# The 96-column remainder of the gate and up projections with x stationary and both weights moving, turned back by a DMA transpose

## The chip, the cores and the metric

The kernel runs on one core of one Trainium2 chip. The metric is the device time of one execution in microseconds (us), given as the median of several runs. The core has a matrix engine (TensorE; PE in the profile, with its weight loads listed apart as PEld), VectorE (DVE), ScalarE (ACT), GpSimd (POOL) and SyncE (SP, whose queue issues nearly all DMAs here). The profile lists each engine's instructions in order of time and, from semaphore events, which engine ended each wait. PSUM is the memory that the matmuls write (PS in the profile); a DMA has *landed* when its data has arrived.

Ratios are the mean time of one kernel's fast runs over the mean of the kernel before in the same rounds on the same chip, so they are not quite the ratio of the medians beside them.

## The reference, cut to what matters

```python
def _B_ref(x, w_gate, w_up, w_down):            # S = 2048 rows, D = 512, F = 1376
    return (_gelu(x @ w_gate) * (x @ w_up)) @ w_down
xn = _layernorm(x)
return x + _A_ref(xn, ...) + _B_ref(xn, w_gate, w_up, w_down)   # _A_ref: a state-space scan
```

F = 1376 is ten tiles of 128 columns and a remainder of 96. The change concerns that remainder in `x @ w_gate` and `x @ w_up`.

## The kernel before

The 2048 rows are worked in four blocks of 512. A gate/up stage computes the hidden layer *transposed*: F on the partitions, rows on the free axis, as the down projection needs it as its stationary operand. A weight tile is stationary (128 columns, or 96 for tile 10) and 512 rows of x move past it. The 96-column tile costs as much as a full one: the trace below has 88 matmuls of 512 moving columns in a stage at 216 ns each, the 8 with 96 stationary columns included.

```python
def GU(b, fts=None):                            # gate/up stage of block b
    def mm(ft, W, Wc, bank, c0, c1, rd):
        m = FROWS[ft]                           # FROWS = [128] * 10 + [96]
        def f(e):
            for dk in range(KD):                # KD = 4: D = 4 * 128
                ins_ = e.matmul(PS[bank][0:m, c0:c1], W.ap[:, dk, 128 * ft:128 * ft + m],
                                XNT[b].ap[:, dk, c0:c1], start=(dk == 0), stop=(dk == KD - 1))
    ... # [cut]
    for ft in fts:
        banks[ft] = (next_bank(), next_bank())  # 8 PSUM banks in turn
        kk = (KF * b + ft) % 3                  # KF = 11; three GG and three UPB buffers
        ... # [cut: 2 x 4 matmuls of 512 moving columns]
        ACT(... GG[kk] <- Gelu(PS[bg]) ...)     # "gelu"
        ACT(... UPB[kk] <- PS[bu] ...)          # "evU"
        V(... HTt[k2][ft] <- GG[kk] * UPB[kk] ...)   # "hmul" on DVE

def TR(b):                                      # input of block b, transposed by DMA
    for j, tt in enumerate(range(4 * b, 4 * b + 4)):
        S.dma(... e.dma_start_transpose(XNT[b].ap[:, :, 128*j:128*(j+1)], XN[tt % 8].ap) ...)

# order of the stages (BU: input of the scan, CHAIN: the scan on DVE, DN: down projection)
GU(0, range(5, KF)); ... BU(1); ... CHAIN(1)
GU(1, range(0, 8)); TR(2); GU(1, range(8, KF)); BU(2); CHAIN(2); DN(0, True)
GU(2, range(0, 8)); TR(3); GU(2, range(8, KF)); BU(3); CHAIN(3); DN(1)
GU(3); DN(2); DN(3)
```

A scheduler in the kernel orders the instructions of ACT, DVE and POOL by priority, but keeps PE and the SP queue in program order (`INORDER = ("tensor", "sync")`). Where a DMA stands in the program text is therefore where it stands in the SP queue.

Of the kernel before, what the change touches and what calls it, by code (L numbers as in the profile page):

```python
# [9 lines left out]
ALU = mybir.AluOpType  # L10
ACTF = mybir.ActivationFunctionType
BF16, F32, I32 = dt.bfloat16, dt.float32, dt.int32
# [332 lines left out]
L, D, P, F = 2048, 512, 512, 1376  # L345
NT, NB, KD, KP, KF = 16, 4, 4, 4, 11
TB_ = 512
FROWS = [128] * 10 + [96]
# [4 lines left out]
def d_pe(n_list):  # L353
    return sum(n / 2.4 + 2.5 for n in n_list)
def d_dve_tt2x(n): return 100.0 + 0.52 * n
def d_dve_1x(n): return 100.0 + 1.04 * n
def d_dve_scan(n): return 90.0 + 2.08 * n
def d_dve_ts4x(n): return 220.0 + 0.26 * n
D_TINY = 160.0
def d_act(n, ptr=0): return 190.0 + 0.833 * n + 90.0 * ptr  # L360
# [3 lines left out]
def build(nc, ins, out):  # L364
    with ExitStack() as es:
        E = es.enter_context
        S = Sched(nc, es)
        ARENA_BYTES = 207 * 1024
        arena_t = E(nc.sbuf_tensor("arena", [128, ARENA_BYTES // 2], BF16))
        A = Arena(arena_t, ARENA_BYTES)  # L370
        PS = [E(nc.psum_tensor("PS%d" % i, [128, 512], F32)) for i in range(8)]
        BANK = [Buf("bank%d" % i, "ps", i, i + 1) for i in range(8)]

        def ring(parent, name, n):
            return [A.sub(parent, "%s%d" % (name, i), i) for i in range(n)]

        WG = A.alloc("WG", [KD, F], BF16)
        WU = A.alloc("WU", [KD, F], BF16)
        WD = A.alloc("WD", [KF, D], BF16)
        FCH = [(0, 384), (384, 896), (896, F)]  # L380
        WGc = [Buf("WGc%d" % i, "sbx", 10 * i, 10 * i + 1) for i in range(3)]
        WUc = [Buf("WUc%d" % i, "sbx", 100 + 10 * i, 101 + 10 * i) for i in range(3)]
        WDc = [Buf("WDc%d" % i, "sbx", 200 + 10 * i, 201 + 10 * i) for i in range(2)]
        XNT_all = A.alloc("XNT", [NB, KD, TB_], BF16)
        XNT = ring(XNT_all, "XNT", NB)
# [28 lines left out]
        XTr = lambda b: XTk[b]  # L414
# [21 lines left out]
        CTMP_all = A.alloc("CTMP", [4, D], F32)  # L436
        CTMP = ring(CTMP_all, "CTMP", 4)
        IOT = A.alloc("IOT", [128], I32)
        SS_all = A.alloc("SS", [3, KP, 2, TB_], BF16); SSb = ring(SS_all, "SS", 3)
        TA = A.alloc("TA", [KP, 2, 512], BF16)  # L440
        TB = A.alloc("TB", [KP, 2, 512], BF16)
# [6 lines left out]
        HTt = [[A.sub(HT[k], "HT%d_%d" % (k, ft), ft) for ft in range(KF)] for k in range(2)]  # L448
# [5 lines left out]
        def ld_x(b):  # L454
            return S.dma(lambda e, b=b: e.dma_start(
                X_all.ap[:, 4 * b:4 * b + 4, :], x2[512 * b:512 * (b + 1), :].rearrange("(j p) d -> p j d", p=128)),
                512 * 1024, writes=X[4 * b:4 * b + 4], tag="ld_x%d" % b)

        def ld_w(W, Wc, src, ci, queue="sync"):
            f0, f1 = FCH[ci]  # L460
            return S.dma(lambda e: e.dma_start(W.ap[:, :, f0:f1], src[:, f0:f1].rearrange("(k p) f -> p k f", p=128)),  # L461
                         512 * (f1 - f0) * 2, writes=[Wc[ci]], tag="ld_w", queue=queue)
# [5 lines left out]
        ld_w(WG, WGc, ins["B_w_gate"], 0)  # L468
        ld_w(WU, WUc, ins["B_w_up"], 0)
        ld_w(WG, WGc, ins["B_w_gate"], 1)  # L470
        ld_w(WU, WUc, ins["B_w_up"], 1)
        for q, nm in enumerate(("A_log_dt", "A_Lambda_re", "A_Lambda_im")):
            S.dma(lambda e, q=q, nm=nm: e.dma_start(PROW.ap[4 * q:4 * q + 4, :], ins[nm].rearrange("(s p) -> s p", p=128)),
                  1024, writes=[PROWq[q]], tag="ld_" + nm, queue="scalar")
        def late_loads():
            S.dma(lambda e: e.dma_start(WD.ap[:, 0:10, :], ins["B_w_down"][0:1280, :].rearrange("(k p) d -> p k d", p=128)),
                  1280 * 1024, writes=[WDc[0]], tag="ld_wd")
            S.dma(lambda e: e.dma_start(WD.ap[0:96, 10, :], ins["B_w_down"][1280:F, :]), 96 * 1024, writes=[WDc[1]], tag="ld_wd")
            ld_x(3)
# [6 lines left out]
        def load_B():  # L486
            ld_x(1)
            load_T([A.sub(BBT_all, "BBTc%d" % c, c) for c in range(2)], ("A_B_re", "A_B_im"))
            ld_w(WG, WGc, ins["B_w_gate"], 2)
            ld_w(WU, WUc, ins["B_w_up"], 2)  # L490
            S.dma(lambda e: e.dma_start(DSKB.ap, ins["A_Dskip"].unsqueeze(0).broadcast_to([128, D])),
# [3 lines left out]
        def load_C():  # L495
            load_T(CRAW, ("A_C_re", "A_C_im"))
# [3 lines left out]
        V = lambda fn, dur, r, w, tag="", after=(): S.op("vector", fn, dur, r, w, tag, after)  # L500
        ACT = lambda fn, dur, r, w, tag="", after=(): S.op("scalar", fn, dur, r, w, tag, after)
        POOL = lambda fn, dur, r, w, tag="": S.op("gpsimd", fn, dur, r, w, tag)
        PE = lambda fn, dur, r, w, tag="": S.op("tensor", fn, dur, r, w, tag)
# [5 lines left out]
        V(lambda e: e.memset(HALF.ap, 0.5), D_TINY, [], [HALF], "half")  # L509
        POOL(lambda e: e.iota(IOT.ap, [[1, 128]], base=0, channel_multiplier=-1), 300, [], [IOT], "iota")  # L510
        V(lambda e: e.tensor_scalar(IDN.ap, IOT.ap, 0.0, None, ALU.is_equal), d_dve_ts4x(128), [IOT], [IDN], "ident")
        POOL(lambda e: e.iota(IOTJ.ap, [[1, 512]], base=0, channel_multiplier=0), 600, [], [IOTJ], "iotj")
        SCR = A.alloc("SCR", [1], F32)
        ACT(lambda e: e.activation(SCR.ap, HALF.ap[:, 0:1], ACTF.Sqrt), 200, [HALF, IOTJ], [SCR], "sqrt0")
        rstate = {"n": 0}

        def next_bank():
            b_ = rstate["n"] % 8
            rstate["n"] += 1
            return b_  # L520
# [24 lines left out]
        GATE = {"before_gelu": [], "nh": 0}  # L545
# [67 lines left out]
        def SKIP(b):  # L613
            for tt in range(4 * b, 4 * b + 4):
                xs = XN[tt % 8]
                V(lambda e, tt=tt, xs=xs: e.tensor_tensor(XD[tt].ap, xs.ap, DSKB.ap, ALU.mult),
                  d_dve_tt2x(512), [xs, DSKB], [XD[tt]], "skip")
# [22 lines left out]
        def TR(b):  # L640
            tts = list(range(4 * b, 4 * b + 4))
            for j, tt in enumerate(tts):
                S.dma(lambda e, b=b, j=j, tt=tt: e.dma_start_transpose(
                    XNT[b].ap[:, :, 128 * j:128 * (j + 1)], XN[tt % 8].ap),
                    1.2 * 128 * 1024, reads=[XN[tt % 8]], writes=[XTk[b][j]], tag="tr_x%d" % b)
# [61 lines left out]
        def GU_first(fts, early, single):  # L707
            banks = [{ft: next_bank() for ft in fts} for h in range(2)]

            def mm(ft, u, j0, j1):  # L710
                W, Wc = ((WG, WGc), (WU, WUc))[u]
                h, q0 = j0 // 2, 256 * u + 128 * (j0 % 2)
# [38 lines left out]
            for ft in fts:  # L751
                for u in range(2):
                    mm(ft, u, 2, 4)
                evac(ft, 1)

        def GU(b, fts=None):
            k2 = b % 2
            fts = list(range(KF) if fts is None else fts)
            banks = {}

            def mm(ft, W, Wc, bank, c0, c1, rd):
                m = FROWS[ft]

                def f(e):
                    ins_ = None
                    for dk in range(KD):
                        ins_ = e.matmul(PS[bank][0:m, c0:c1], W.ap[:, dk, 128 * ft:128 * ft + m], XNT[b].ap[:, dk, c0:c1],  # L767
                                        start=(dk == 0), stop=(dk == KD - 1))
                    return ins_
                PE(f, d_pe([c1 - c0] * 4), [Wc[wchunk(ft)]] + rd, [BANK[bank]], "GU%d" % b)  # L770

            for ft in fts:
                m = FROWS[ft]
                banks[ft] = (next_bank(), next_bank())
                bg, bu = banks[ft]
                kk = (KF * b + ft) % 3
                for (W, Wc, bank) in zip((WG, WU), (WGc, WUc), banks[ft]):
                    mm(ft, W, Wc, bank, 0, 512, XTr(b))
                GATE["last_gelu"] = ACT(lambda e, bg=bg, kk=kk, m=m: e.activation(  # L779
                    GG[kk].ap[0:m, :], PS[bg][0:m, :], ACTF.Gelu_apprx_tanh),  # L780
                    d_act(512), [BANK[bg]], [GG[kk]], "gelu", after=GATE["before_gelu"])
                ACT(lambda e, bu=bu, kk=kk, m=m: e.activation(UPB[kk].ap[0:m, :], PS[bu][0:m, :], ACTF.Copy),  # L782
                    d_act(512), [BANK[bu]], [UPB[kk]], "evU")
                V(lambda e, kk=kk, m=m, ft=ft, k2=k2: e.tensor_tensor(  # L784
                    HTt[k2][ft].ap[0:m, :], GG[kk].ap[0:m, :], UPB[kk].ap[0:m, :], ALU.mult),
                  d_dve_tt2x(512), [GG[kk], UPB[kk]], [HTt[k2][ft]], "hmul")

        def DN(b, split=False):
# [18 lines left out]
            def hidden(j):  # L807
                ops = [(HTt[k2][ft].ap[0:FROWS[ft], :], WD.ap[0:FROWS[ft], ft, :]) for ft in range(KF)]
                mms(j, ops, False, [HTt[k2][ft] for ft in range(KF)] + WDc)
# [53 lines left out]
        LN(1); SKIP(1)  # L863
        TR(1)
        load_C()
        GU(0, range(5, KF))
        late_loads()
        BU(1)
        coefs()
        scale_C()  # L870
        CHAIN(1)
        LN(2); SKIP(2)
        GU(1, range(0, 8)); TR(2); GU(1, range(8, KF))
        BU(2)
        CHAIN(2)
        DN(0, True)
        LN(3); SKIP(3)
        GU(2, range(0, 8)); TR(3); GU(2, range(8, KF))
        BU(3)
        CHAIN(3)  # L880
        DN(1)
        GU(3)
        DN(2)
        DN(3)

# [56 lines left out]
```

## Time and profile before

| | before |
|---|---|
| median | 182.26 us (3 runs), 182.19 us over 6 runs of two calls |
| span of the profiled run | 180.7 us |
| PE busy | 97% |
| gate/up stage, 88 matmuls | 19.0 us |
| tile 10 of one block, 8 matmuls of 512 columns | 1.73 us |

The profile's page, kernel before: busy time by engine, and the chain of work that ended last.

```profile
PE 174.4 (97%) x865; PEld 84.2 (47%) x880; DVE 156.7 (87%) x270; ACT 93.9 (52%) x170; POOL 9.7 (5%) x20
...
PE 93%; DMA 3%; SPq 1%; issue 1%; DVE 0%; DVEq 0%
```

The waits of PE (who waited for whom, us in total, times, longest).

```profile
PE PS L839 <- DVE arena L509: 1.0, 1, 1.0
PE PS L718 <- DVE arena L609: 0.7, 1, 0.7
PE PS L718 <- DMA arena<-in_B_w_up_dram: 0.6, 1, 0.6
PE PS L630 <- DVE arena L609: 0.2, 1, 0.2
```

They add up to 2.5 us (the prediction's "about 3 us" is rough) and belong to the first 9 us. Afterwards PE waits for nothing: the kernel is bound by the columns that stream through PE.

The timeline of PE (start, length, line, operation, count). L767 is the gate/up stage, L655 the Bu stage, L802 the down projection.

```profile
83.34 19.16 PE L767 MATMUL PS<-arena 128*128 128x512 bf16 x87
102.33 7.07 PE L655 MATMUL PS<-arena 128*128 128x512 bf16 x31
...
125.66 19.16 PE L767 MATMUL PS<-arena 128*128 128x512 bf16 x87
144.66 33.00 PE L802 MATMUL PS<-arena 128*128 128x512 bf16 x149
```

Read start to start: from 125.66 to 144.66 are 19.00 us for 88 matmuls (one record is missing), 216 ns each. The length of a merged line is longer, since the record of one such matmul lasts 379 ns, more than the 216 ns to the next start. Eight of these, tile 10, are 1.73 us.

Shorter matmuls occur in the early stage. The view by windows there (window, length, PE busy and number of matmuls, granted clock, DMA share, GB/s):

```profile
8.30:10.70 2.40, 2.40 (x40) 1.00 1.07 371
11.30:17.00 5.70, 5.70 (x53) 1.00 1.20 213
```

The first window is not pure. Kept apart by shape (`--lines --by-form`), it holds:

```profile
L718 PE MATMUL PS<-arena 128*128 128x128 bf16 x36 | 2.2, 219 | 0.6 <-DMA arena<-in_B_w_up_dram 0.6
L718 PE MATMUL PS<-arena 128*128 128x256 bf16 x4 | 0.6, 272 | 0.0
```

With 109 ns for the four of 256 columns, the 36 of 128 columns take 56 ns each: start to start the 40 fill 2.45 us, from 8.27 to 10.72. The next eight, all of 128 columns, run from 10.72 to 11.17, again 56 ns each.

The SP queue in the timeline: the DMA transposes for the inputs of blocks 2 and 3.

```profile
36.81 7.27 SPq L643 DMA_TRANSPOSE arena<-arena  x4
...
84.64 6.18 SPq L643 DMA_TRANSPOSE arena<-arena  x4
```

The last of each four landed at 45.8 and 92.1 us. The Bu stages that read them begin near 60.0 and at 102.33 us, so they have some 14 and 10 us to spare.

### The profile page before, as it was taken

How to read it: one execution, taken by the hardware profiler on the slowest of the kernel's cores; microseconds unless marked ns; L12 is line 12 of the kernel's file. 1: busy time of each engine (PE TensorE's matmuls, PEld its weight loads, DVE VectorE, ACT ScalarE, POOL GpSimd, SP SyncE). 2: the span in 40 equal slices, each digit the busy share in tenths (PEclk: the TensorE clock that was granted, in tenths of full speed). 3: DMA queues.
4: the chain of work that ended last, by engine and by line, in shares of the span. 5: the costliest groups of instructions: out<-in, count | busy, mean ns of one | idle time of the engine just before them, and what ended most of it. 6: DMA issues, size and time to landing. Idle time of an engine off the chain costs nothing.

```text
span 180.7 us, 2411 instructions
## 1 busy us (share of the span) xinstructions
PE 174.4 (97%) x865; PEld 84.2 (47%) x880; DVE 156.7 (87%) x270; ACT 93.9 (52%) x170; POOL 9.7 (5%) x20
## 2 busy tenths in 40 slices
PE   7699999999999999999999999999999999999993
PEld 3497444444444444444444444444444444444441
DVE  4779996998989989988999999999989999998111
ACT  4497999876666899002667793000667701700000
POOL 2200112042000000200000000000000000000000
PEclk9999999999999999999999999999999999999999
DMA  5999925999000000002410000000000000003100
GB/s 127 293 326 176 317 46 113 173 314 252 1 0 4 0 0 0 0 31 89 89 29 0 2 0 4 29 29 29 29 0 0 4 0 0 0 0 116 62 29 29
DMA packets 24067, 12.38 MB, mean 68 GB/s; under 512 B 15384, under 2 KB 24056, under 8 KB 24056
## 3 DMA queue, kind: packets, MB, share of 16 engines
q1 hardware_dynamic: 24032, 12.23, 27.5%
q8 instruction: 7, 0.11, 0.3%
q14 instruction: 4, 0.03, 0.1%
q10 hardware_dynamic: 24, 0.00, 0.0%
HBM read 6.46 MB, written 2.10 MB: 47 GB/s over the span
## 4 chain that ended last, share of the span: by engine, by line
PE 93%; DMA 3%; SPq 1%; issue 1%; DVE 0%; DVEq 0%
PE PS L767 37%; PE PS L802 36%; PE PS L655 15%; PE PS L718 5%; DMA arena<-in_B_w_up_dram 3%; SPq L465 1%; DVE arena L818 0%; PE PS L630 0%; SPq L461 0%; DVEq L331 0%
## 5 line engine op out<-in xcount | busy, mean ns | idle before, releaser
L767 PE MATMUL PS<-arena 128*128 128x512 bf16 (+1 forms) x308 | 67.8, 379 | 0.2
L802 PE MATMUL PS<-arena 128*128 128x512 bf16 (+1 forms) x297 | 65.8, 379 | 0.4
L767 PEld LDWEIGHTS PS<-arena 128*128 128x128 bf16 (+1 forms) x312 | 31.4, 100 | 36.1
L779 ACT ACTIVATE arena<-PS 128x512 bf16<-128x512 f32 (+1 forms) x39 | 23.5, 603 | 46.2 <-PE PS L767 36.8
L802 PEld LDWEIGHTS PS<-arena 128*128 128x128 bf16 (+1 forms) x304 | 29.7, 98 | 36.0
L688 DVE TENSOR_TENSOR_SCAN arena<-arena 128x512 bf16<-128x512 f32 x32 | 38.9, 1255 | 0.9 <-POOL arena L536 0.9
L655 PE MATMUL PS<-arena 128*128 128x512 bf16 x124 | 27.7, 379 | 0.2
L782 ACT ACTIVATE arena<-PS 128x512 bf16<-128x512 f32 (+1 forms) x39 | 23.5, 602 | 7.2 <-PE PS L767 7.1
L818 DVE TENSOR_TENSOR arena<-PS,arena 128x512 bf16<-128x512 f32 x16 | 10.6, 681 | 10.7 <-PE PS L802 10.7
L655 PEld LDWEIGHTS PS<-arena 128*128 128x128 bf16 x128 | 12.5, 98 | 14.8
L659 ACT ACTIVATE arena<-PS 128x512 bf16<-128x512 f32 x32 | 17.9, 592 | 2.7 <-PE PS L655 2.6
L784 DVE TENSOR_TENSOR arena<-arena 128x512 bf16<-128x512 bf16 (+1 forms) x39 | 15.5, 414 | 3.6 <-ACT arena L782 3.3
L596 DVE BATCH_NORM_STATS2 arena<-arena 128x6 f32<-128x512 bf16 x16 | 10.3, 682 | 1.4 <-DMA arena<-in_A_x_dram 1.3
L718 PE MATMUL PS<-arena 128*128 128x256 bf16 (+1 forms) x104 | 9.5, 248 | 1.3 <-DVE arena L609 0.7
L794 ACT ACTIVATE PS<-arena 128x512 f32<-128x512 bf16 x16 | 9.4, 602 | 0.7
L677 DVE TENSOR_TENSOR arena<-arena 128x4096 bf16<-128x4096 bf16 (+1 forms) x5 | 9.3, 1856 | 0.0
L675 DVE TENSOR_TENSOR arena<-arena 128x4096 bf16<-128x4096 bf16 (+1 forms) x5 | 9.3, 1855 | 0.0
L700 DVE TENSOR_TENSOR arena<-arena 128x4096 bf16<-128x4096 bf16 x4 | 9.1, 2287 | 0.0
L701 DVE TENSOR_TENSOR arena<-arena 128x4096 bf16<-128x4096 bf16 x4 | 9.1, 2284 | 0.0
L718 PEld LDWEIGHTS PS<-arena 128*128 128x128 bf16 x104 | 8.1, 98 | 2.1 <-DMA arena<-in_B_w_gate_dram 0.8
L609 DVE TENSOR_SCALAR arena<-arena 128x512 bf16<-128x512 bf16 x16 | 5.9, 409 | 0.4
L572 DVE SCALAR_TENSOR_TENSOR arena<-arena 128x512 bf16<-128x512 bf16 x8 | 5.6, 747 | 0.7 <-ACT arena L569 0.7
(81 smaller groups left out, 89.4 us busy)
## 6 DMA issues: line engine op xcount, KB each, us to landing
out_dram<-arena SPq DMA_DIRECT2D x16, 128.0 KB, 1.7
arena<-in_A_x_dram SPq DMA_DIRECT2D x3, 512.0 KB, 7.6
arena<-in_B_w_down_dram SPq DMA_DIRECT2D x1, 1280.0 KB, 7.0
arena<-in_A_x_dram SPq DMA_DIRECT2D x4, 128.0 KB, 2.2
arena<-in_B_w_gate_dram SPq DMA_DIRECT2D x1, 512.0 KB, 5.9
arena<-in_B_w_up_dram SPq DMA_DIRECT2D x1, 512.0 KB, 6.8
arena<-in_B_w_gate_dram SPq DMA_DIRECT2D x1, 480.0 KB, 4.2
arena<-in_B_w_up_dram SPq DMA_DIRECT2D x1, 480.0 KB, 5.1
```

What stands on the lines that cost most here:

```text
L596: V(lambda e, tt=tt: e.bn_stats(ST[tt].ap, X[tt].ap), d_dve_1x(512), [X[tt]], [ST[tt]], "bnst", after)
L655: ins_ = e.matmul(PS[bank][:, :], BBT[c][dk].ap[:, 128 * s:128 * (s + 1)], XNT[b].ap[:, dk, :], start=(dk == 0), stop=(dk == KD - 1))
L659: ACT(lambda e, bank=bank, k3=k3, s=s, c=c: e.activation(SSc[k3][s][c].ap, PS[bank][:, :], ACTF.Copy), d_act(512), [BANK[bank]], [SSc[k3][ ...
L688: V(lambda e, g=g, rb=rb, init=init: e.tensor_tensor_scan(g.ap, rb, g.ap, init, ALU.mult, ALU.add), d_dve_scan(512), [g, PA[RRr]] + ([CARc ...
L718: ins_ = e.matmul(PS[bank][:, q0:q0 + 128 * (j1 - j0)], W.ap[:, dk, 128 * ft:128 * (ft + 1)], XNT[0].ap[:, dk, 128 * j0:128 * j1], start=( ...
L767: ins_ = e.matmul(PS[bank][0:m, c0:c1], W.ap[:, dk, 128 * ft:128 * ft + m], XNT[b].ap[:, dk, c0:c1], start=(dk == 0), stop=(dk == KD - 1))
L779: GATE["last_gelu"] = ACT(lambda e, bg=bg, kk=kk, m=m: e.activation(GG[kk].ap[0:m, :], PS[bg][0:m, :], ACTF.Gelu_apprx_tanh), d_act(512), ...
L782: ACT(lambda e, bu=bu, kk=kk, m=m: e.activation(UPB[kk].ap[0:m, :], PS[bu][0:m, :], ACTF.Copy), d_act(512), [BANK[bu]], [UPB[kk]], "evU")
L784: V(lambda e, kk=kk, m=m, ft=ft, k2=k2: e.tensor_tensor(HTt[k2][ft].ap[0:m, :], GG[kk].ap[0:m, :], UPB[kk].ap[0:m, :], ALU.mult), d_dve_tt ...
L794: ACT(lambda e: e.activation(PS[bank][:, :], X[tt].ap, ACTF.Copy), d_act(512), [X[tt]], [BANK[bank]], "seed")
L802: ins_ = e.matmul(PS[bank][:, :], l_[:, 128 * j:128 * (j + 1)], r_, start=False, stop=last and n == len(ops) - 1, skip_group_check=True)
L818: V(lambda e: e.tensor_tensor(OUTB[ko].ap, PS[bank][:, :], XD[tt].ap, ALU.add), d_dve_1x(512), [BANK[bank], XD[tt]], [OUTB[ko]], "evO")
```

## The change

The intent: exchange the operands for the remainder. With 128 rows of x stationary and the 96 columns of *both* weights moving side by side, one matmul moves 192 columns and wastes none. A block needs 4 row groups x 4 depth tiles = 16 such matmuls: 16 x 192 = 3072 columns instead of 8 x 512 = 4096. The result has rows on the partitions, so it must be transposed before the down projection. A DMA does that, from a small buffer HR with its unused columns set to zero. The remainder is moved forward in each stage, to give the DMA time.

```diff
+        assert WG.lo == 0 and WU.lo == WG.hi
+        WGU = arena_t[:, 0:2 * KD * F].rearrange("p (w k f) -> p w k f", w=2, k=KD)
+        HR = A.alloc("HR", [4, 128], BF16)            # [cut: two halves HRp; memset once on POOL]
+        def GU_rest(b):
+            k2, ft = b % 2, KF - 1
+            f0, m = 128 * ft, FROWS[ft]
+            for i in range(2):
+                bank = next_bank()
+                # [cut: head of the function given to PE]
+                    for j in (2 * i, 2 * i + 1):
+                        dst = PS[bank][:, 256 * (j % 2):256 * (j % 2) + 2 * m].rearrange(...)
+                        for dk in range(KD):
+                            ins_ = e.matmul(dst, XNT[b].ap[:, dk, 128 * j:128 * (j + 1)],
+                                            WGU[:, :, dk, f0:f0 + m], start=(dk == 0), stop=(dk == KD - 1))
+                GATE["nh"] = kk = (GATE["nh"] + 1) % 3
+                ... # [cut: gelu, evU (2 x 96 columns each), hmul into HR]
+            S.dma(lambda e: e.dma_start_transpose(HTt[k2][ft]..., HR.ap), reads=HRp, writes=[HTt[k2][ft]], ...)
         ... # in GU: if m < 128: GU_rest(b); continue
-        GU(0, range(5, KF))
+        GU(0, [5, 10, 6, 7, 8, 9])
-        GU(1, range(0, 8)); TR(2); GU(1, range(8, KF))
+        GU(1, [0, 1, 2, 10, 3, 4, 5, 6, 7]); TR(2); GU(1, [8, 9])
-        GU(2, range(0, 8)); TR(3); GU(2, range(8, KF))
+        GU(2, [0, 1, 2, 10, 3, 4, 5, 6, 7]); TR(3); GU(2, [8, 9])
-        GU(3)
+        GU(3, [0, 1, 2, 10, 3, 4, 5, 6, 7, 8, 9])
```

More of the change, by code (lines that the diff above doesn't have):

```diff
@@ L438, in build @@
         IOT = A.alloc("IOT", [128], I32)
+        HR = A.alloc("HR", [4, 128], BF16)
+        HRp = [A.sub(A.alloc("HRv", [2, 256], BF16, at=HR.lo), "HR%d" % i, i) for i in range(2)]
         SS_all = A.alloc("SS", [3, KP, 2, TB_], BF16); SSb = ring(SS_all, "SS", 3)
@@ L514, in build @@
         ACT(lambda e: e.activation(SCR.ap, HALF.ap[:, 0:1], ACTF.Sqrt), 200, [HALF, IOTJ], [SCR], "sqrt0")
+        POOL(lambda e: e.memset(HR.ap, 0.0), 300, [], HRp, "hr0")
         rstate = {"n": 0}
@@ L754, in GU_first, with f @@
                 evac(ft, 1)
+        def GU_rest(b):
[3 more added lines that the diff above has]
+                bank = next_bank()
+                def f(e, i=i, bank=bank):
+                    ins_ = None
+                    for j in (2 * i, 2 * i + 1):
+                        dst = PS[bank][:, 256 * (j % 2):256 * (j % 2) + 2 * m].rearrange("p (w f) -> p w f", w=2)
+                        for dk in range(KD):
+                            ins_ = e.matmul(dst, XNT[b].ap[:, dk, 128 * j:128 * (j + 1)], WGU[:, :, dk, f0:f0 + m],
+                                            start=(dk == 0), stop=(dk == KD - 1))
+                    return ins_
+                PE(f, d_pe([2 * m] * 8), [WGc[2], WUc[2]] + XTr(b), [BANK[bank]], "GR%d" % b)
+                GATE["nh"] = kk = (GATE["nh"] + 1) % 3
+                g_, u_ = (PS[bank][:, :].rearrange("p (j x) -> p j x", j=2)[:, :, w * m:(w + 1) * m] for w in range(2))
+                gs, us = (t[kk].ap[:, 0:2 * m].rearrange("p (j f) -> p j f", j=2) for t in (GG, UPB))
+                GATE["last_gelu"] = ACT(lambda e, g_=g_, gs=gs: e.activation(gs, g_, ACTF.Gelu_apprx_tanh),
+                                        d_act(2 * m), [BANK[bank]], [GG[kk]], "gelu", after=GATE["before_gelu"])
+                ACT(lambda e, u_=u_, us=us: e.activation(us, u_, ACTF.Copy), d_act(2 * m), [BANK[bank]], [UPB[kk]], "evU")
+                V(lambda e, i=i, gs=gs, us=us: e.tensor_tensor(HR.ap[:, 2 * i:2 * i + 2, 0:m], gs, us, ALU.mult),
+                  d_dve_tt2x(2 * m), [GG[kk], UPB[kk]], [HRp[i]], "hmul")
+            S.dma(lambda e: e.dma_start_transpose(HTt[k2][ft].ap.rearrange("p (j t) -> p j t", j=4), HR.ap),
+                  1.2 * 128 * 1024, reads=HRp, writes=[HTt[k2][ft]], tag="tr_h%d" % b, issue=1200.0)
         def GU(b, fts=None):
@@ L773, in GU @@
                 m = FROWS[ft]
+                if m < 128:
+                    GU_rest(b)
+                    continue
                 banks[ft] = (next_bank(), next_bank())
```

## The prediction

> **What bounds it now.** TensorE. The busy table has PE at 97% of a 180.7 us span (DVE 87%, ACT 52%), the chain that ended last is 93% PE, and PE's waits add up to about 3 us, all before 9 us. In the timeline PE runs from 17.1 us to the end without a gap. So time leaves only if PE columns leave and nothing new makes PE wait.
>
> **Removed.** In each of four blocks the 96-column remainder (ft 10) takes 8 matmuls of 512 columns. In the timeline a gate/up stage of 88 matmuls runs from 125.66 to 144.66 us: 216 ns each, so 1.73 us for the remainder.
>
> **Put in.** 16 matmuls of 192 moving columns, each with a 128-column weight load. The trace has neighbours: early, 40 matmuls of 128 columns fill 2.40 us (60 ns each) and 53 of 256 fill 5.70 us (108 ns). That fits the Trainium skill ("TensorE: Matmul & The Clock Gate", section "Back-to-back issue gap": columns/2.4 + 2.5 ns, so 216, 109 and 56). Estimate for 192 between those neighbours: 83 ns, 1.33 us per block. Weight loads stay hidden, as 60 ns was sustained with one load each. Gain: 0.40 us a block, 1.6 us in all, all on the critical path.
>
> **Moved.**
> - ACT: two 512-wide evictions (0.60 us) become four of 192 (estimate 0.33 each). The new pieces share the three GG/UPB buffers out of step: the remainder's first Gelu gets the buffer of the tile just before it, and the next tile that of its second half. ACT therefore waits for hmul on DVE, up to about 2 us in block 2 behind scans of 1.28 us. Eight PSUM banks give PE some 6.9 us of lead, so I expect no PE wait.
> - DVE: one hmul (pitch 0.34 us) becomes two of 192, about the same.
> - The DMA transpose (issue 1.27 us, landing 2.5 us for this size in the trace) sits in the in-order SP queue *ahead* of the transposes of the next block's input. These were issued at 36.8 and 84.6 us; now they wait for the remainder's hmul, about 48.7 and 91.8 us by the DVE order with trace durations. Four at 1.3 us plus landing: in place by about 57 and 99.5 us; the Bu stages that read them should start at 59.4 and 101.1 us. Margin 1.5 to 2 us: used up, not exceeded.
> - Block 3: DVE ends its hmuls at 158.4 us, PE needs them at 161.1, now about 159.6. Margin about 1 us.
>
> **Predicted: 180.7 us** (182.26 - 1.6), range 180.1 to 182.2. Chances: faster by over 2% 0.01, within 2% 0.96, slower by over 2% 0.03.
>
> **What would show each step.** PE gaps only at the start; each full gate/up stage 18.6 us instead of 19.0; the 192-column group at 82 to 85 ns start to start. Input transposes issued some 13 us (block 1's end) and 8 us (block 2's end) later, yet no PE wait for a DMA. ACT's Gelu waiting for hmul. DN stages unchanged at 216 ns per matmul.
>
> **What would make it wrong.** (1) A PE wait for the late input transposes at the third or fourth Bu stage: a remainder hmul 2 us later than estimated costs PE directly and could cancel the gain (about 15%). (2) 192-column matmuls bound by weight loads or by the two-piece moving pattern: at 95 ns the gain falls to 0.8 us, at 108 ns to nothing. (3) DVE slipping by over 1 us in block 3, so that DN(3) waits. (4) A gain below the spread of the runs (0.7 us over three), so the median may show between 1 and 2 us.

## The result, and the profile after

| | before | after |
|---|---|---|
| median of 6 runs | 182.19 us (181.78 to 182.46) | 180.67 us (180.35 to 180.87) |
| ratio of fast runs | 1 | 0.9914, 95% interval 0.9897 to 0.9931 |
| span of the profiled run | 180.7 us | 179.0 us |
| gate/up stage of blocks 1, 2, 3 | 19.0 us each | 18.6 us each |

The two sets of runs do not overlap, and the interval excludes 1. The page of the changed kernel, the same lines as before:

```profile
PE 173.9 (97%) x896; PEld 86.0 (48%) x912; DVE 156.9 (88%) x274; ACT 92.5 (52%) x178; POOL 10.1 (6%) x21
...
PE 94%; DVE 2%; ACT 1%; issue 1%; DVEq 0%
```

The shares are the same, as PE is as full as before, only for a shorter time. The waits of PE, again all in the early stage:

```profile
PE PS L873 <- DVE arena L513: 1.0, 1, 1.0
PE PS L723 <- DVE arena L610: 0.2, 1, 0.2
```

The chain in order of time (start, length, what), in block 3. L772 is the remainder, L798 the full tiles.

```profile
124.60 5.18 PE PS L798 x24
129.78 1.32 PE PS L772 x16
```

The next full tile starts at 131.15 us. The remainder takes 1.32 us, which is 82 ns per matmul, where its eight predecessors took 1.73. The windows of the four gate/up stages, starting with block 0 (which has only six tiles here); first the kernel before, then the changed one:

```profile
23.75:34.12 10.37, 10.32 (x49) 1.00 0.74 116
41.02:60.01 18.99, 18.94 (x88) 1.00 0.30 55
83.34:102.33 18.99, 18.94 (x88) 1.00 0.20 43
125.66:144.66 19.00, 18.95 (x89) 1.00 0.02 8
sum 67.35, PE 67.14; mean PE 16.78
```

```profile
23.75:33.70 9.95, 9.90 (x56) 1.00 0.66 94
40.61:59.20 18.59, 18.49 (x96) 1.00 0.47 93
82.52:101.11 18.59, 18.48 (x96) 1.00 0.22 51
124.44:143.02 18.58, 18.48 (x95) 1.00 0.06 15
sum 65.71, PE 65.34; mean PE 16.34
```

The sums differ by 1.64 us, about the whole difference of the two spans (1.7 us). Nothing is lost or gained elsewhere in this pair of traces, which happen to reach the first of these windows at the same time, 23.75 us.

What moved in the SP queue (L784 is the new transpose, L648 the input transposes):

```profile
48.72 1.20 SPq L784 DMA_TRANSPOSE arena<-arena  x1
49.96 5.67 SPq L648 DMA_TRANSPOSE arena<-arena  x4
...
91.73 1.20 SPq L784 DMA_TRANSPOSE arena<-arena  x1
92.97 5.19 SPq L648 DMA_TRANSPOSE arena<-arena  x4
```

The input transposes are now issued 13 and 8 us later than before. The last of the first group, issued at 53.9 us, landed 3.2 us later at 57.1. That of the second, issued at 96.9, landed 2.5 us later at 99.4. The Bu stages began at 59.20 and 101.11 us. So 2.1 and 1.7 us were left (1.7 and 1.7 in a second trace of this kernel, f1_after below).

The waits of ACT for hmul that the shared buffers bring (L779 is the remainder's Gelu, L813 that of a full tile; L782 and L818 are their hmuls):

```profile
ACT arena L813 <- DVE arena L782: 2.1, 2, 1.7
...
ACT arena L779 <- DVE arena L818: 1.0, 2, 0.5
```

They exist, as foreseen, and PE does not wait for ACT anywhere.

### The profile page after: what moved, and what is told of

It is laid out like the page before. It is cut to its first block, busy times and chain, and to the rows that moved or that the text cites. A ratio compares the mean times of both kernels' runs of the same rounds, so it can differ in the third digit from the quotient of the medians.

```text
span 179.0 us, 2485 instructions
## 1 busy us (share of the span) xinstructions
PE 173.9 (97%) x896; PEld 86.0 (48%) x912; DVE 156.9 (88%) x274; ACT 92.5 (52%) x178; POOL 10.1 (6%) x21
## 4 chain that ended last, share of the span: by engine, by line
PE 94%; DVE 2%; ACT 1%; issue 1%; DVEq 0%
PE PS L836 36%; PE PS L798 34%; PE PS L660 15%; PE PS L772 3%; PE PS L873 3%; PE PS L723 3%; ACT L731 1%; DVE arena L601 1%; DVE arena L643 0%; DVE arena L852 0%; DVE arena L735 0%; PE PS L635 0%; DVE arena L614 0%; ACT arena L731 0%; ACT arena L605 0%
## 5 line engine op out<-in xcount | busy, mean ns | idle before, releaser
L836 PE MATMUL PS<-arena 128*128 128x512 bf16 (+1 forms) x297 | 65.8, 379 | 0.4
L798 PE MATMUL PS<-arena 128*128 128x512 bf16 x273 | 60.7, 379 | 0.4
L836 PEld LDWEIGHTS PS<-arena 128*128 128x128 bf16 (+1 forms) x304 | 29.6, 97 | 36.0
L813 ACT ACTIVATE arena<-PS 128x512 bf16<-128x512 f32 x35 | 21.0, 601 | 46.7 <-PE PS L798 33.5
L798 PEld LDWEIGHTS PS<-arena 128*128 128x128 bf16 x280 | 27.3, 98 | 32.1
L660 PE MATMUL PS<-arena 128*128 128x512 bf16 x126 | 28.0, 379 | 0.1
L816 ACT ACTIVATE arena<-PS 128x512 bf16<-128x512 f32 x35 | 21.0, 600 | 5.3 <-PE PS L798 5.2
L660 PEld LDWEIGHTS PS<-arena 128*128 128x128 bf16 x128 | 12.5, 98 | 14.9
L664 ACT ACTIVATE arena<-PS 128x512 bf16<-128x512 f32 x32 | 17.8, 593 | 2.6 <-PE PS L660 2.5
L818 DVE TENSOR_TENSOR arena<-arena 128x512 bf16<-128x512 bf16 x35 | 13.7, 415 | 2.8 <-ACT arena L816 2.6
L723 PEld LDWEIGHTS PS<-arena 128*128 128x128 bf16 x104 | 8.0, 97 | 1.3 <-DVE arena L542 0.4
```

The costliest lines, as they stand in the source:

```text
L660: ins_ = e.matmul(PS[bank][:, :], BBT[c][dk].ap[:, 128 * s:128 * (s + 1)], XNT[b].ap[:, dk, :], start=(dk == 0), stop=(dk == KD - 1))
L664: ACT(lambda e, bank=bank, k3=k3, s=s, c=c: e.activation(SSc[k3][s][c].ap, PS[bank][:, :], ACTF.Copy), d_act(512), [BANK[bank]], [SSc[k3][ ...
L723: ins_ = e.matmul(PS[bank][:, q0:q0 + 128 * (j1 - j0)], W.ap[:, dk, 128 * ft:128 * (ft + 1)], XNT[0].ap[:, dk, 128 * j0:128 * j1], start=( ...
L813: GATE["last_gelu"] = ACT(lambda e, bg=bg, kk=kk, m=m: e.activation(GG[kk].ap[0:m, :], PS[bg][0:m, :], ACTF.Gelu_apprx_tanh), d_act(512), ...
L816: ACT(lambda e, bu=bu, kk=kk, m=m: e.activation(UPB[kk].ap[0:m, :], PS[bu][0:m, :], ACTF.Copy), d_act(512), [BANK[bu]], [UPB[kk]], "evU")
L818: V(lambda e, kk=kk, m=m, ft=ft, k2=k2: e.tensor_tensor(HTt[k2][ft].ap[0:m, :], GG[kk].ap[0:m, :], UPB[kk].ap[0:m, :], ALU.mult), d_dve_tt ...
```

## The experiments

The theory: PE is bound by streamed columns; the change takes 1024 columns out of each block, and everything it adds fits beside PE. Rivals: the gain comes from the new order of tiles, from another weight load or eviction pattern, or is larger but partly paid for by the transpose. A second question is how close the kernel came to a new wait.

### The new order alone (e1_order)

```diff
 # kernel before, operands unchanged; only the order of the tiles as in the change
-        GU(0, range(5, KF))
+        GU(0, [5, 10, 6, 7, 8, 9])
 ... # [cut: GU(1), GU(2), GU(3) likewise]
```

> The kernel before with only the new order of the gate/up tiles (the remainder second in block 0, fourth in blocks 1 to 3); operands as before, no transpose. Columns theory: PE streams the same columns, so 182.2 us, ratio to before 0.998 to 1.002. Rival (the gain comes from the new order of tiles and of DVE work): some 180.7 us, ratio 0.991.

Measured: 182.47 us, ratio 1.0004 (0.9986 to 1.0023). The order by itself is worth nothing.

### 256 moving columns instead of 192 (e2_256)

```diff
-  e.matmul(dst, XNT[b]..., WGU[:, :, dk, f0:f0 + m], ...)      # dst: 2 * m = 192 columns
+  e.matmul(dst, XNT[b]..., WGU[:, :, dk, F - 128:F], ...)      # dst: 256 columns
-  ... [:, :, w * m:(w + 1) * m]                                # what gelu and evU read
+  ... [:, :, 128 * w + 32:128 * w + 128]
```

> The changed kernel, but the moving operand is the last 128 columns of each weight instead of the last 96, so 256 columns per matmul; evictions, hmul and DMA transpose stay 96 wide and the result is right. Columns theory: 16 matmuls of 108 ns are 1.73 us a block, as much as the 8 of 512 they replace, so the whole gain goes: 182.2 us, ratio 0.998 to 1.002. Rival (the gain comes from anything else that the change did: other weight loads, other evictions, other order): stays near 180.7, ratio 0.991 to 0.993.

Measured: 182.46 us, ratio 1.0025 (0.999 to 1.006; one of six runs was 184.42), result right. The timeline of PE:

```profile
88.12 1.91 PE L772 MATMUL PS<-arena 128*128 128x256 bf16 x16
89.87 12.25 PE L798 MATMUL PS<-arena 128*128 128x512 bf16 x56
```

16 matmuls in 1.75 us, 109 ns each. Everything else of the change is there, and the gain is gone. So the gain is the 64 columns per matmul that this run put back.

### 96 moving columns, wrong result (e3_96)

```diff
-            f0, m = 128 * ft, FROWS[ft]
+            f0, m = 128 * ft, 48
```

> The changed kernel with 96 moving columns (48 of each weight) instead of 192; wrong result on purpose. If columns alone set the pace, 16 matmuls of about 43 ns: 0.68 us a block, 178.1 us, ratio 0.978. If each pair of weight load and matmul has a floor of 60 ns (the 128-column pace of the trace): 0.96 us a block, 179.3 us, ratio 0.984. Start to start in the trace tells which.

Measured: 178.32 us, ratio 0.9784 (0.9766 to 0.9803). The timeline:

```profile
86.27 0.84 PE L772 MATMUL PS<-arena 128*128 128x96 bf16 x16
86.95 12.25 PE L798 MATMUL PS<-arena 128*128 128x512 bf16 x56
```

16 in 0.68 us: 42.5 ns each, each with its own 128-column weight load. The pace by columns holds down to 96; there is no 60 ns floor from weight loads (and 60 ns was not the 128-column pace, see above). The Trainium skill's formula ("TensorE: Matmul & The Clock Gate", section "Back-to-back issue gap": columns/2.4 + 2.5 ns) gives 42.5, 55.8, 82.5, 109.2 and 215.8 ns for 96, 128, 192, 256 and 512 columns. These traces show 42.5, 56, 82, 109 and 216.

### No DMA transpose, wrong result (e4_nodma)

```diff
-            S.dma(lambda e: e.dma_start_transpose(HTt[k2][ft]..., HR.ap), ...)
+        for k in range(2):                       # once, at the start
+            POOL(lambda e, k=k: e.memset(HTt[k][KF - 1].ap, 0.0), ...)
```

> The changed kernel without its four DMA transposes; tile 10 of HT is set to zero once at the start, so the result is wrong on purpose. Theory (the transposes are off the critical path): 180.7 us, ratio 0.990 to 0.993, the same as with them. Rival (they cost something by the SP queue or by DMA contention): faster than the changed kernel by 0.3 us or more, ratio under 0.989.

Measured: 180.84 us, ratio 0.9919 (0.9903 to 0.9935), which is the changed kernel's time. The four transposes cost nothing that the time shows.

### The remainder four tiles later (e5_late)

```diff
-        GU(1, [0, 1, 2, 10, 3, 4, 5, 6, 7]); TR(2); GU(1, [8, 9])
+        GU(1, [0, 1, 2, 3, 4, 5, 6, 10, 7]); TR(2); GU(1, [8, 9])
 ... # [cut: GU(2) likewise]
```

> The changed kernel with the remainder at the eighth place instead of the fourth in blocks 1 and 2, still ahead of the input transposes in the SP queue. Theory (the queue order has a cost that the early place only just avoided): the remainder's hmul ends some 6.5 us later in block 1, the four input transposes land at 63 to 64 us, and the third Bu stage waits 4 to 5 us for them; the fourth waits 3.5 to 6 us. Time 188 to 192 us, with PE waits for the transposes at these two places. Rival (place in the queue does not matter): 180.7 us and no PE wait.

Measured: 191.13 us, ratio 1.0471 (1.0449 to 1.0492). The waits of PE have a new first line, and the timeline shows the places:

```profile
PE PS L660 <- DMA arena<-arena: 7.3, 2, 3.7
```

```profile
53.77 5.34 PE L798 MATMUL PS<-arena 128*128 128x512 bf16 x24
62.68 9.98 PE L660 MATMUL PS<-arena 128*128 128x512 bf16 x32 [3.57 <-DMA arena<-arena]
72.49 16.58 PE L836 MATMUL PS<-arena 128*128 128x512 bf16 x76
...
102.32 5.34 PE L798 MATMUL PS<-arena 128*128 128x512 bf16 x24
111.37 7.07 PE L660 MATMUL PS<-arena 128*128 128x512 bf16 x32 [3.71 <-DMA arena<-arena]
118.28 16.58 PE L836 MATMUL PS<-arena 128*128 128x512 bf16 x76
```

The queue order has the cost that the theory gives it, though the third Bu stage waited a little less than the 4 to 5 us expected. But the total lay in the expected range partly for a reason that was not foreseen. Start to start, the two Bu stages began 3.7 and 3.9 us later than the matmuls before them called for (24 matmuls of 216 ns are 5.18 us). That is 7.6 us of the 10.5 by which this kernel is slower than the changed one. The other 2.9 us are in the first of the two Bu stages itself: 9.81 us from its start to the next stage's, where the second takes 6.91. The windows tell why (granted clock in the third column of numbers after the length):

```profile
62.68:68.00 5.32, 5.32 (x13) 0.50 0.00 0
68.00:69.00 1.00, 1.00 (x4) 0.70 0.00 0
69.00:72.40 3.40, 3.40 (x17) 1.00 0.00 0
111.40:118.20 6.80, 6.80 (x32) 1.00 0.01 2
```

After the first wait PE ran at half its clock for about 5.9 us (a mean of 0.70 in the window from 68 to 69 us puts the change at 68.6). After the second, slightly longer wait it kept its full clock. The Trainium skill ("TensorE: Matmul & The Clock Gate", section "What's actually happening") says that the clock falls to half after at least one idle window of about 3.4 us, and that this window runs free of the program. That would allow one wait of this length to hold a whole idle window and another not to. The traces fit it, but no run here varied the phase, so this stays the likely reason and not a shown one. The loss was not the same in every run either: three of the four had a mean granted clock of 0.982, one had 0.989 and was 0.9 us faster (190.21 us). Only one of the four, with 0.982, has a trace.

### The same late place behind the input transposes (e6_trfirst)

```diff
-        GU(1, [0, 1, 2, 3, 4, 5, 6, 10, 7]); TR(2); GU(1, [8, 9])     # e5_late
+        TR(2); GU(1, [0, 1, 2, 3, 4, 5, 6, 10, 7]); GU(1, [8, 9])
 ... # [cut: TR(3) and GU(2) likewise]
```

> The same late place of the remainder as e5_late, but the input transposes are put into the SP queue before the gate/up stage, so ahead of the remainder's transpose. Theory: the waits of e5_late come from the queue order alone, so none here: 180.7 us, ratio 0.990 to 0.993, input transposes issued at about 37 and 84 us as in the kernel before. Rival (the late remainder itself is what hurts): as slow as e5_late.

Measured: 180.68 us, ratio 0.991 (0.9896 to 0.9923). The SP queue:

```profile
37.69 6.82 SPq L648 DMA_TRANSPOSE arena<-arena  x4
54.90 1.19 SPq L784 DMA_TRANSPOSE arena<-arena  x1
...
83.55 5.12 SPq L648 DMA_TRANSPOSE arena<-arena  x4
97.62 1.19 SPq L784 DMA_TRANSPOSE arena<-arena  x1
```

The new transpose of block 1 is issued as late as in e5_late (54.90 and 54.91 us), and nobody waits. The late remainder does no harm; only its place in the queue does.

### The remainder two tiles later (f3_late2)

```diff
-        GU(1, [0, 1, 2, 10, 3, 4, 5, 6, 7]); TR(2); GU(1, [8, 9])
+        GU(1, [0, 1, 2, 3, 4, 10, 5, 6, 7]); TR(2); GU(1, [8, 9])
 ... # [cut: GU(2) likewise]
```

> The remainder two tiles later (sixth place) in blocks 1 and 2, still ahead of the input transposes. In e5_late the last input transpose landed 7.6 us after the remainder's transpose was issued. Theory: it is issued at about 51.9 us, so the third Bu stage waits 0.3 to 0.8 us, the fourth 0 to 0.7 us, and as these waits are short the granted clock stays at 1.00: 181.2 to 182.2 us, ratio 0.994 to 0.999. Rival (the margin is larger than I think): 180.7 us, no wait.

Measured: 182.58 us, ratio 1.0019 (1.0004 to 1.0033): the whole gain is gone, and a little more than expected. The waits of PE:

```profile
PE PS L660 <- DMA arena<-arena: 1.5, 2, 1.2
```

The new transpose was issued at 52.03 us, as expected. The third Bu stage waited 1.24 us, not 0.3 to 0.8, because one of the input transposes held the queue for 2.07 us instead of 1.27. The fourth waited 0.25 us. Start to start these are 1.4 and 0.4 us, together the 1.8 us by which this trace is longer than that of f1_after (the changed kernel on the same chip, below) from the first 512-column gate/up matmul to the end. The clock stayed at 1.00. The margin of the changed kernel is thus about as small as its trace says: two tiles of delay are enough to eat the gain.

### Transpose on TensorE instead of by DMA (e7_petr, f2_petr)

```diff
-            S.dma(lambda e: e.dma_start_transpose(HTt[k2][ft]..., HR.ap), ...)
+            # put into the PE stream three tiles later
+            for j in range(4):
+                ins_ = e.transpose(pt[0:m, 128 * j:128 * (j + 1)], HR.ap[:, j, 0:m], IDN.ap)
+            ACT(... HTt[k2][ft].ap[0:m, :] <- pt[0:m, 0:512] ...)
```

> The changed kernel with four TensorE transposes of 128 columns per block and one ScalarE eviction in place of the DMA transpose. PE transposes took 56 ns each in the early stage of the trace, so 0.23 us a block, 0.9 us in all: 181.6 us, ratio 0.996, over half of the gain given back. Rival (PE has slack for them, or the DMA route has a hidden cost of its own): ratio 0.991 or less.

Measured: 181.13 us, ratio 0.9939 (0.9926 to 0.9953). That gives back 0.5 us, while its trace has 0.9 us more PE work than the changed kernel. In its profiled run the first 512-column gate/up matmul came at 23.06 us instead of 23.75. Over the profiled runs that point lies anywhere from 23.06 to 23.87 us, although the PE program up to there is the same. To settle whether the TensorE route really shortens the early stage, the kernel was run again beside the changed one (f1_after):

> The changed kernel again, as the measure for the next run on the same chip: ratio 0.990 to 0.993. From the start of the first 512-column gate/up matmul to the end of the span: 155.2 us, whatever the early stage took.

> e7_petr again, since its time gave back 0.5 us where its trace shows 0.9 us more of PE work. Theory (early-stage scatter): from the first 512-column gate/up matmul to the end 156.1 us, 0.9 more than the changed kernel, and a ratio 0.9 us above that of f1_after, so 0.995 to 0.997. Rival (the TensorE route really shortens the early stage): ratio again 0.994 or less and the first 512-column gate/up matmul again some 0.5 us earlier than in f1_after.

Measured: f1_after 180.69 us, ratio 0.9916 (0.9902 to 0.9929); f2_petr 181.51 us, ratio 0.9956 (0.9942 to 0.997). From the first 512-column gate/up matmul to the end of the span it is 178.8 - 23.54 = 155.3 us for f1_after and 179.5 - 23.36 = 156.1 us for f2_petr. The four transposes of a block take 0.22 us in the timeline of f2_petr:

```profile
94.27 0.39 PE L792 MATMUL PS<-arena 128*96 128x128 bf16 x4
94.49 7.07 PE L809 MATMUL PS<-arena 128*128 128x512 bf16 x31
```

So the TensorE route costs 0.9 us as costed, over half of the gain. In the trace of e7_petr the same stretch is 179.2 - 23.06 = 156.1 us too: that execution was better only by its early stage. The other runs of e7_petr have no trace, so for them the early stage is the likely reason and not a shown one. In f2_petr the first 512-column matmul came 0.2 us before that of f1_after, not 0.5.

### In turn for all buffers (e9_best)

```diff
 # e6_trfirst, and in GU:
-                kk = (KF * b + ft) % 3
+                GATE["nh"] = kk = (GATE["nh"] + 1) % 3
```

> e6_trfirst with the three GG/UPB buffers handed out in turn to all tiles, so that no Gelu waits for the hmul of the tile just before it. Theory: ACT's waits for hmul shrink from some 3 us to under 1 us, and the time does not move, since PE never waited for them: 180.7 us, ratio 0.990 to 0.993. Rival (these waits reach PE): 180.2 us or less.

Measured: 180.52 us, ratio 0.9904 (0.989 to 0.9917). The waits between the remainder and its neighbours, to which the shared buffers lead, are 3.1 us in the changed kernel (2.1 and 1.0 in the lines above), 0.6 us in e6_trfirst and 0.3 us in e9_best. The later place of the remainder had thus removed most of them before the buffers were handed out anew, and the expected "some 3 us" was the changed kernel's. From 3.1 to 0.6 to 0.3 us the time did not move by more than the intervals. No version is clearly faster than the changed kernel; e6_trfirst and e9_best are as fast and have their input transposes back at 38 and 84 us.

## Why the prediction was right or wrong

The predicted 180.7 us met a measured 180.67, and the steps behind it held. The gain was predicted as 1.6 us and measured as 1.5 by the medians and 1.64 by the traces; that the totals agree to 0.03 us, far less than the spread of the runs (0.5 us or more), is luck.

- **The bound.** PE columns set the time. e1_order, e2_256 and e3_96 show it from three sides: same columns, same time (1.0004); columns put back, gain gone (1.0025); columns halved, gain of 2.2% (0.9784).
- **The size.** Predicted 83 ns per 192-column matmul and 0.40 us per block; measured 82 ns and 0.41. The estimate lay between two neighbours in the same trace, of which one was misread: the 60 ns at 128 columns came from a window with four matmuls of 256 in it, and are 56. Halfway between 60 and 108 is 84 ns, between 56 and 109 it is 82.5, so the slip could move the total by no more than 0.1 us. The skill's formula gives 82.5 too.
- **Weight loads hidden.** Right, with more room than the prediction claimed (its 60 ns were 56): e3_96 sustained 42.5 ns with a load each.
- **ACT and DVE.** The small evictions took 0.33 us each, as estimated; two hmul of 0.25 us took the place of one of 0.41. ACT waits for hmul of up to 1.7 us appeared where expected (predicted about 2) and never reached PE; e6_trfirst has a fifth of these waits, e9_best a tenth, and neither is clearly faster. In block 3 DVE ended its hmuls at 158.5 us. By its start at 143.02 us and 76 matmuls of 216 ns before it, DN(3) needed them at 159.4. The margin was 0.9 us, predicted about 1.
- **The SP queue.** The new transposes were predicted at 48.7 and 91.8 us and issued at 48.72 and 91.73. The margin was predicted as 1.5 to 2 us and measured as 2.1 and 1.7. e5_late, e6_trfirst and f3_late2 show that the risk named there was real and that it is the queue order that carries it.
- **What the risk was worth.** The prediction said that a hmul 2 us later than estimated could cancel the gain. By the measured margins (2.1 and 1.7 us) 2 us more would hardly have cost anything; no run tried it. In f3_late2 the transposes were issued 3.3 us later, and that cancelled the gain (1.0019). So the risk was real, but it was put too close. What it did not foresee is that a longer wait can cost beyond itself: 2.9 us at half clock in e5_late.

Not settled: whether the clock fell in e5_late after one wait and not the other because of the phase of the idle window, and what makes the early stage scatter by 0.8 us.

## What to carry to other kernels

When a matmul-bound kernel has a tile that does not fill the stationary side, count moving columns for both choices of operands: 16 x 192 in place of 8 x 512 saved 25% of that tile's columns and 24% of its time (1.73 to 1.32 us). Count too who pays for the transpose that follows: by DMA it was free here, on TensorE it gave back 0.9 of 1.6 us. Before you take a pace from a window, see which shapes are in it. A DMA put into an in-order queue delays every DMA behind it by the wait in front of it, so put those that depend on nothing recent ahead of it. If the effect is under one per cent, compare traces from a mark behind the scattered start, not only whole times.

## What the Trainium skill lacked or had wrong

- "TensorE: Matmul & The Clock Gate", section "Back-to-back issue gap": it says that in a real kernel pairs of weight load and matmul sustain about 81 ns at 128 columns and 131 ns at 512, and calls columns/2.4 + 2.5 the isolated figure. Here the pairs sustain 56 ns at 128 columns, 82 at 192, 109 at 256, 216 at 512, and 42.5 at 96; the formula is the better guide.
- The same page, "What's actually happening", gives about 3.4 us of activity for the return to full clock. In e5_late it took about 5.9 us of back-to-back matmuls, at a cost of 2.9 us; a wait of similar length elsewhere in that run cost none. As the page says "at least one" window and lets it run free, this need not contradict it, but 3.4 us alone would put the loss too low.
- The same page, section "LDWEIGHTS (loading the stationary operand)": its formula (columns/1.2 ns) makes a 96-column load shorter than a 128-column one. The trace of the kernel before has 123 ns for 96 columns and 98 ns for 128. The section "Weight-path perf modes", which ties the fast load to 128 columns, fits that.
- The same page, "Part 4: PE-mode transpose", gives some 275 to 390 ns for one transpose of 128 x 128, and no pace for several. In f2_petr (96 columns by 128) one record lasts 219 ns, and four back to back take 0.22 us of PE's time.
- "DMA: Bandwidth & Descriptors" has no time for which one DMA transpose of 128 x 512 two-byte elements within SBUF holds the issuing queue (the nearest is a count of sequencer cycles for 8,192 tiles, whose size it does not give). Here it is mostly 1.2 to 1.27 us each, up to 2.25 in the kernel before and 2.41 in f1_after, with mostly 2.5 us to landing, and up to 7.6 in the kernel before beside the loads of w_down and x. That time in the queue is what made the place in it matter.
